# Single-query cached attention: K's loads move from SP's DMA queue to GpSimd's, one packet per DMA engine and load

## The chip, the cores and the metric

One NeuronCore of a Trainium2 chip runs the whole kernel. The metric is device time in microseconds for one execution, the lower the better. Three runs of the kernel before took 2513.58 (the median), 2513.52 and 2514.34 us. About 0.2% (5 us) is what a measurement of this kernel can tell from no change.

## The reference

One decode step: a gated mix of a cached multi-head attention (32 heads, head size 128, 65536 cached positions, one query) and a small SwiGLU block. All inputs are bfloat16.

```python
# x: [1, 1, 512]; k_cache, v_cache: [1, 32, 65536, 128]; wq: [512, 4096]; wo: [4096, 512]
q = (x @ wq) per head                                  # [1, 32, 1, 128]
p = softmax(einsum("bhqd,bhkd->bhqk", q, k_cache) * 128 ** -0.5)
a = einsum("bhqk,bhkd->bhqd", p, v_cache) as [1, 1, 4096] @ wo
b = (silu(x @ w_gate) * (x @ w_up)) @ w_down           # w_gate, w_up: [512, 1792]
g = sigmoid((x * gate_w).sum())
out = g * a + (1 - g) * b                              # [1, 1, 512]
```

Nearly all bytes are K and V: 32 heads x 2 x 16.8 MB = 1073.7 MB, of 1087.6 MB in all.

## The kernel before, in words

Each head's K and each head's V (16.8 MB) is loaded in two halves, u = 0 and u = 1 (called K_A, K_B and V_A, V_B here, with the head in brackets: K_A(r+1)). A half is 128 partitions x 64 KB = 8.39 MB, one DMA. A row is one partition's 64 KB. All four kinds lie in one buffer, `ring`, of 176 KB per partition, and overlap there: K_A is at 0 to 64 KB, K_B at 32 to 96 KB, V_A at 96 to 160 KB, V_B at 112 to 176 KB. So a half may be loaded only when enough of the half that lies across it has been used.

What each engine does for head r, in its order:

- VectorE (DVE) turns K: it waits for K_A(r), transposes it in 16 chunks into four small buffers `kt` (L314, semaphore `ktd` counts the chunks, 32 per head), then copies `psW` into `brow` (L327) and scales `psO` (L330), which ends the head before; then it waits for K_B(r), turns its 16 chunks, takes the maximum of the scores (L338) and transposes the probabilities (L340).
- TensorE (PE) makes four score matmuls per chunk (L401). After the scores of K_A(r) it works off V_B(r-1): 48 matmuls from `flow` (L417), 8 that add up `brow` (L452), 64 from `values` (L408), after which `vbd` goes up. After the scores of K_B(r) and the softmax it works off V_A(r): 48 matmuls of `flow`, after which `va1` goes up, and 16 more. PE works strictly in this order: scores of K_A(r+1) stand behind V_A(r), scores of K_B(r+1) behind V_B(r). DVE can be four chunks ahead of PE, no more.
- ScalarE (ACT) makes the exponentials, GpSimd (POOL) the two reductions over partitions per head (L216, L218), which wait for `s_mx` and `s_exp`.
- SP issues every large DMA, in one queue and in this order per head (function `head`, L167): K_A(r+1) once 8 chunks of K_B(r) are turned, V_B(r) once `va1` says that most of V_A(r) is used, K_B(r+1) once 8 chunks of K_A(r+1) are turned, V_A(r+1) once `vbd` says that V_B(r) is used. In the last such head, the two loads of `wo` stand between V_B and K_B.

The start is a special case: the query weights `wq` (4.19 MB) are issued first (L136), then head 0's K in four halves of a half. The row of x and the gate's row come through ACT's queue (L137, L232), 1 KB each. V_A(0) lies over `wq` and waits until the query is made (`s_q`). At the end, after the `wo` matmuls of heads 0 to 30 (L428, L512; semaphore `s_wod`), come the SwiGLU weights and V_B(31) in six pieces.

Of the kernel before, what the change touches and what calls it, by code (L numbers as in the profile page):

```python
# [9 lines left out]
K_A, K_B = 0, 32 * KB  # L10
# [16 lines left out]
def bass_gated_mix__mha_block_cached__swiglu_ffn__decode_kernel(  # L27
# [11 lines left out]
    out: bass.AP,  # L39
):  # L40
    _, H, S, Dh = A_k_cache.shape
    D = A_wq.shape[0]
    F = B_w_gate.shape[1]
    Dc = D // P
    FC = F // P
    ROWS = S // (2 * P)
    NCH = ROWS // CH
    SCALE = float(Dh) ** -0.5
    assert Dh == 128 and D == 512 and F % P == 0 and ROWS == 256 and H == 32
    L = H - 1  # L50
    A_ORDER = list(range(NCH // 2, NCH)) + list(range(NCH // 2))
    B_ORDER = list(range(NCH))
    PER = 2 * NCH

    with ExitStack() as ctx:
# [6 lines left out]
        def sem(name):  # L62
            return ctx.enter_context(nc.semaphore(name))
# [47 lines left out]
        sm = {n: sem(n) for n in names.split()}  # L111
# [4 lines left out]
        kv_dram = {"k": A_k_cache[0].rearrange("h (u p r) d -> h u p (r d)", u=2, p=P),  # L116
                   "v": A_v_cache[0].rearrange("h (u p r) d -> h u p (r d)", u=2, p=P)}

        def at(byte, n):
            return ring[:, byte // 2:byte // 2 + n]  # L120
# [21 lines left out]
        @block.sync  # L142
        def _(sp):
            def load(dst, src, s):
                sp.dma_start(dst, src).then_inc(sm[s], 16)  # L145

            def place(kind, h, u, s):
                byte = {"k": (K_A, K_B), "v": (V_A, V_B)}[kind][u]
                src = kv_dram[kind][:, u]
                if isinstance(h, int):  # L150
                    src = src[h]
                else:
                    src = src[bass.ds(h, 1)].rearrange("h p n -> (h p) n")
                load(at(byte, ROWS * Dh), src, s)

            k0 = kv_dram["k"][0, 0]
            k1 = kv_dram["k"][0, 1]
            half = ROWS * Dh // 2
            load(at(K_A + 2 * half, half), k0[:, half:2 * half], "s_ka")
            load(at(K_A, half), k0[:, 0:half], "s_k0a")  # L160
            load(at(K_B + 2 * half, half), k1[:, half:2 * half], "s_k0b")
            sp.wait_ge(sm["ktd"], NCH // 2)
            load(at(K_B, half), k1[:, 0:half], "s_kb")
            sp.wait_ge(sm["s_q"], 1)
            place("v", 0, 0, "s_va")

            def head(r, late):  # L167
                sp.wait_ge(sm["ktd"], r * PER + (PER - NCH // 2))
                place("k", r + 1, 0, "s_ka")
                sp.wait_ge(sm["va1"], r + 1)  # L170
                place("v", r, 1, "s_vb")
                if late:
                    wo_dram = A_wo.rearrange("(p j) n -> p (j n)", j=32)
                    for q in range(2):
                        sp.wait_ge(sm["ktd"], r * PER + (PER + 3 * NCH // 4 + q * NCH // 4))
                        load(at(WO + q * 16 * KB, 16 * D), wo_dram[:, q * 16 * D:(q + 1) * 16 * D], "s_wo")
                sp.wait_ge(sm["ktd"], r * PER + (PER + NCH // 2))
                place("k", r + 1, 1, "s_kb")
                sp.wait_ge(sm["vbd"], r + 2)
                place("v", r + 1, 0, "s_va")  # L180

            with nc.Fori(0, L - 1, engines=[ET.SP]) as i:
                head(i, False)
            head(L - 1, True)
            sp.wait_ge(sm["s_wod"], 1)
            load(at(WG, Dc * F), B_w_gate.rearrange("(p c) f -> p (c f)", c=Dc), "s_wg")
            load(at(WU, Dc * F), B_w_up.rearrange("(p c) f -> p (c f)", c=Dc), "s_wu")
            sp.wait_ge(sm["ktd"], PER * H)
            wd_dram = B_w_down.rearrange("(p c) n -> p (c n)", c=FC)
            load(at(WD, WD_CUT * D), wd_dram[:, 0:WD_CUT * D], "s_wd")  # L190
            last = kv_dram["v"][L, 1]
            for n, ((r0, r1), s) in enumerate(zip(PARTS, MARKS)):
                if n == 1:
                    sp.wait_ge(sm["va1"], H)
                load(at(V_B + r0 * 256, (r1 - r0) * Dh), last[:, r0 * Dh:r1 * Dh], s)
            for j, s in ((FC - 3, "s_wd1"), (FC - 2, "s_wd2"), (FC - 1, "s_wd3")):
                load(at(WD + 2 * j * D, D), wd_dram[:, j * D:(j + 1) * D], s)

        @block.gpsimd
        def _(pool):  # L200
            nc.gpsimd.memset(xTz[:], 0.0).then_inc(sm["s_qd"], 1)
            nc.gpsimd.memset(qd[:], 0.0).then_inc(sm["s_qd"], 1)
            for m, n in enumerate(MARKS[1:]):
                nc.gpsimd.memset(hbuf[:, m], 0.0).then_inc(sm[n], 16 * L)
            nc.gpsimd.memset(hot[:], 0.0).then_inc(sm["s_hot"], 1)
            pool.wait_ge(sm["s_id"], 1)
            pool.wait_ge(sm["s_hot"], 1)
            nc.gpsimd.tensor_copy(hot[:, 31:128:32], ident[:, P - 4:P])
            for je in range(4):
                off = 64 * (je // 2) + je % 2  # L210
                last = nc.gpsimd.tensor_copy(sel[:, je, :].rearrange("p (g d) -> p g d", g=4),
                                             ident[:, off:off + 63:2].unsqueeze(1).to_broadcast([P, 4, 32]))
            last.then_inc(sm["s_sel"], 1)
            for h in range(H):
                pool.wait_ge(sm["s_mx"], h + 1)
                nc.gpsimd.partition_all_reduce(amx, mxs, P, RMAX).then_inc(sm["s_ar"], 1)  # L216
                pool.wait_ge(sm["s_exp"], h + 2)
                nc.gpsimd.partition_all_reduce(Lt, rsum, P, RADD).then_inc(sm["s_L"], 1)  # L218

        @block.scalar  # L220
        def _(act):
# [342 lines left out]
```

## Time and profile before

| | |
|---|---|
| median of the runs | 2513.58 us (2513.52 to 2514.34) |
| the profiled execution, first to last instruction (span) | 2512.5 us |
| bytes read from HBM | 1087.64 MB, 433 GB/s over the span |
| busy share: PE, DVE, ACT, POOL | 60%, 50%, 2%, 1% |
| one head in the steady part | 77.27 us (1221.80 to 1299.07, from the issue of one K_A to that of the next) |
| granted TensorE clock, mean | 0.785 |

The page of the profile has one time for the profiled execution, its span of 2512.5 us; the 1.1 us to the median of the runs lie outside of the span. Rows of the timeline read: start, duration, engine, line, operation, output<-input, count, and in brackets how long the engine had been idle and what released it. A row SPq is a DMA issue: its duration is that of the issue, not of the transfer. In the table of stretches the columns are the stretch, its length, each engine's busy time with its count, the granted clock, the busy share of the 16 DMA engines and the rate in GB/s.

### The profile page before, as it was taken

The numbers are of one execution on the slowest core, as the hardware profiler recorded it, in microseconds if no ns is written. First come the engines' busy times: TensorE is split into PE (matmuls) and PEld (weight loads), VectorE is DVE, ScalarE is ACT, GpSimd is POOL, SyncE is SP. The second block draws the span as 40 slices with busy tenths as digits, with TensorE's granted clock in tenths as the row PEclk, the third lists the DMA queues.
The fourth block names the chain that finished last, engine by engine and source line by source line (L and its number), as shares of the span: only waits on it lengthen the run. The fifth ranks groups of instructions, "written<-read, shape, count | busy, mean of one in ns | idle before, by whom it ended". The sixth has DMA issues, their size and how long they took to land.

```text
span 2512.5 us, 25250 instructions
## 1 busy us (share of the span) xinstructions
PE 1510.1 (60%) x10158; PEld 574.4 (23%) x10158; DVE 1249.7 (50%) x1213; ACT 43.0 (2%) x142; POOL 25.9 (1%) x81
## 2 busy tenths in 40 slices
PE   5565655755656556566465565565655655656568
PEld 1222221222222222222222221222221222222222
DVE  5464553644545536446455364464553644645534
ACT  0000000000000000000000000000000000000000
POOL 0000000000000000000000000000000000000000
PEclk9877877878778777778787787777877777778779
DMA  9999999999999999999999999999999999999999
GB/s 418 434 434 434 434 434 434 434 434 434 434 434 434 434 434 434 434 434 434 434 434 434 434 434 434 436 435 435 435 435 435 434 434 435 434 436 434 434 433 395
DMA packets 20749, 1087.73 MB, mean 433 GB/s; under 512 B 2308, under 2 KB 2695, under 8 KB 2951
## 3 DMA queue, kind: packets, MB, share of 16 engines
q1 hardware_dynamic: 20736, 1087.64, 100.0%
q8 instruction: 4, 0.07, 0.0%
q14 instruction: 3, 0.02, 0.0%
q10 hardware_dynamic: 6, 0.00, 0.0%
HBM read 1087.64 MB, written 0.00 MB: 433 GB/s over the span
## 4 chain that ended last, share of the span: by engine, by line
DMA 75%; DVE 15%; issue 7%; PE 2%; DVEq 0%; SPq 0%; ACT 0%; POOL 0%
DMA ring<-in_A_k_cache_dram 74%; DVE kt L314 15%; PE psS L401 2%; DMA ring<-in_A_v_cache_dram 1%; DVEq L311 0%; SPq L145 0%; PE psW L417 0%; DVE st L325 0%; PE psY L423 0%; ACT pa L251 0%; DVE pb L340 0%; DVE st L338 0%; DVEq L324 0%; DVE fin L359 0%; SPq L136 0%
## 5 line engine op out<-in xcount | busy, mean ns | idle before, releaser
L401 PE MATMUL psS<-kt,zq 128*128 128x512 bf16 x4096 | 1132.7, 426 | 851.7 <-DVE kt L314 833.2
L314 DVE STREAM_TRANSPOSE kt<-ring 128x1024 uint32<-128x1024 uint32 x1024 | 1163.1, 1206 | 936.4 <-DMA ring<-in_A_k_cache_dram 936.4
L401 PEld LDWEIGHTS psS<-kt,zq 128*128 128x128 bf16 x4096 | 386.8, 104 | 1583.9 <-DVE kt L314 1120.7
L417 PE MATMUL psW<-ring,pb 128*4 128x512 bf16 x3584 | 253.5, 444 | 103.5 <-DVE pb L340 102.4
L417 PEld LDWEIGHTS psW<-ring,pb 128*4 128x4 bf16 x3584 | 93.9, 97 | 261.3 <-issue 184.4
L327 DVE COPY brow<-psW 128x512 f32<-128x512 f32 x32 | 22.1, 691 | 120.3 <-PE psW L417 120.3
L408 PEld LDWEIGHTS psO<-pb,ring 128*128 128x128 bf16 x2048 | 56.8, 98 | 0.6 <-DMA ring<-in_A_v_cache_dram 0.6
L408 PE MATMUL psO<-pb,ring 128*128 128x1 bf16 x2048 | 56.5, 163 | 0.4 <-DMA ring<-in_A_v_cache_dram 0.2
L330 DVE TENSOR_SCALAR lt<-psO,st,sc 128x4 f32 x32 | 9.4, 294 | 89.1 <-PE psO L408 89.1
L452 PE MATMUL psO<-id,brow 128*128 128x1 f32 x256 | 33.7, 253 | 25.6 <-DVE brow L327 24.8
L340 DVE STREAM_TRANSPOSE pb<-pa 128x512 bf16<-128x512 bf16 x32 | 22.8, 711 | 48.7 <-ACT pa L251 48.7
L249 ACT ACTIVATE st<-st 128x1 f32<-128x1 f32 x32 | 6.5, 203 | 2353.9 <-POOL st L216 2353.9
L338 DVE TENSOR_REDUCE st<-psS 128x1 f32<-128x512 f32 x32 | 22.1, 692 | 37.4 <-PE psS L401 37.4
L452 PEld LDWEIGHTS psO<-id,brow 128*128 128x128 f32 x256 | 31.0, 191 | 41.7 <-DVE brow L327 40.4
L216 POOL PARTITION_ALL_REDUCE st<-st x32 | 11.2, 351 | 2416.5 <-DVE st L338 2416.5
L251 ACT ACTIVATE pa<-psS,st 128x512 bf16<-128x512 f32 x32 | 22.0, 687 | 1.0
L428 PE MATMUL psF<-ring,om 128*1 (+1 forms) x32 | 13.1, 410 | 2.7 <-DMA ring<-in_A_wo_dram 2.7
L512 PE MATMUL psY<-ring,hot 128*128 (+1 forms) x32 | 13.6, 424 | 0.0
L218 POOL PARTITION_ALL_REDUCE st<-st x32 | 12.3, 384 | 36.4 <-ACT pa L251 36.4
L256 ACT COPY zq<-qd 128x16 bf16 x31 | 7.7, 248 | 0.0
L251 ACT ACTIVATION_READ_ACCUMULATOR pa<-psS,st 128x1 f32 x32 | 6.2, 193 | 0.0
L428 PE MATMUL psF<-ring,kt 128*1 128x512 bf16 x11 | 4.0, 542 | 2.9 <-DVE kt L353 2.9
(87 smaller groups left out, 53.2 us busy)
## 6 DMA issues: line engine op xcount, KB each, us to landing
ring<-in_A_k_cache_dram SPq DMA_DIRECT2D x4, 4096.0 KB, 27.5
ring<-in_A_v_cache_dram SPq DMA_DIRECT2D x3, 2048.0 KB, 17.3
ring<-in_A_wq_dram SPq DMA_DIRECT2D x1, 4096.0 KB, 12.3
ring<-in_A_wo_dram SPq DMA_DIRECT2D x2, 2048.0 KB, 10.5
ring<-in_B_w_gate_dram SPq DMA_DIRECT2D x1, 1792.0 KB, 20.6
ring<-in_B_w_up_dram SPq DMA_DIRECT2D x1, 1792.0 KB, 24.4
ring<-in_B_w_down_dram SPq DMA_DIRECT2D x1, 1408.0 KB, 12.8
ring<-in_A_v_cache_dram SPq DMA_DIRECT2D x1, 1280.0 KB, 20.8
```

The lines of the kernel that those rows point to most:

```text
L218: nc.gpsimd.partition_all_reduce(Lt, rsum, P, RADD).then_inc(sm["s_L"], 1)
L251: nc.scalar.activation(pa[:], psS[:], ACT.Exp, bias=nbias, scale=SCALE, accum_out=rsum).then_inc(sm["s_exp"], 1)
L314: nc.vector.transpose(o, src).then_inc(sm["ktd"], 1)
L327: nc.vector.tensor_copy(brow[:], psW[:]).then_inc(sm["s_flc"], 1)
L338: nc.vector.reduce_max(mxs, psS[:], AX_X).then_inc(sm["s_mx"], 1)
L340: nc.vector.transpose(pb[:], pa[:]).then_inc(sm["s_pb"], 1)
L401: last = nc.tensor.matmul(psS[:], zw[je][c], ktb[n % NB][:, je // 2, :, je % 2], start=first and je == 0, stop=stop and je == 3)
L408: last = nc.tensor.matmul(psO[:, 0:1], at(base + r * 256, Dh), pb[:, col:col + 1], start=first and n == 0, stop=stop and n == len(rows) - 1)
L417: last = nc.tensor.matmul(psW[g:g + 4, :], pb[:, col:col + 97:32], at(base + r * 256, 4 * Dh), start=first and n < 4, stop=stop and n >= l ...
L428: return nc.tensor.matmul(psF[0:1, :], lhs, rhs, start=first, stop=stop)
L452: nc.tensor.matmul(psO[:, 0:1], brow[:, e * Dh:(e + 1) * Dh], id4[:, e:e + 1], start=e == 0, stop=False)
L512: return nc.tensor.matmul(psY[:], hot[:, bass.ds(31 - j, P)], w, start=first, stop=stop)
```

## The change

The loads of K, but for two of the four pieces of head 0's K, are taken from SP's program and put into GpSimd's, each behind the same wait as before, and with `single_packet=True`: on each of the 16 DMA engines, one load of 8 rows (512 KB) is asked to be one packet. SP keeps `wq`, two pieces of head 0's K, all of V, and the other weights. So there are now two queues with large loads, where there was one.

```diff
@@ block.sync
-            load(at(K_A + 2 * half, half), k0[:, half:2 * half], "s_ka")
             load(at(K_A, half), k0[:, 0:half], "s_k0a")
             load(at(K_B + 2 * half, half), k1[:, half:2 * half], "s_k0b")
-            sp.wait_ge(sm["ktd"], NCH // 2)
-            load(at(K_B, half), k1[:, 0:half], "s_kb")
             sp.wait_ge(sm["s_q"], 1)
             place("v", 0, 0, "s_va")
 
             def head(r, late):
-                sp.wait_ge(sm["ktd"], r * PER + (PER - NCH // 2))
-                place("k", r + 1, 0, "s_ka")
                 sp.wait_ge(sm["va1"], r + 1)
                 place("v", r, 1, "s_vb")
...
-                sp.wait_ge(sm["ktd"], r * PER + (PER + NCH // 2))
-                place("k", r + 1, 1, "s_kb")
                 sp.wait_ge(sm["vbd"], r + 2)
                 place("v", r + 1, 0, "s_va")
@@ block.gpsimd
+            def k_load(dst, src, s):
+                nc.gpsimd.dma_start(dst, src, single_packet=True).then_inc(sm[s], 16)
+
+            half = ROWS * Dh // 2
+            k_load(at(K_A + 2 * half, half), kv_dram["k"][0, 0, :, half:2 * half], "s_ka")
             nc.gpsimd.memset(xTz[:], 0.0).then_inc(sm["s_qd"], 1)
...
+            pool.wait_ge(sm["ktd"], NCH // 2)
+            k_load(at(K_B, half), kv_dram["k"][0, 1, :, 0:half], "s_kb")
             for h in range(H):
+                if h < L:
+                    pool.wait_ge(sm["ktd"], h * PER + (PER - NCH // 2))
+                    k_load(at(K_A, ROWS * Dh), kv_dram["k"][h + 1, 0], "s_ka")
                 pool.wait_ge(sm["s_mx"], h + 1)
                 nc.gpsimd.partition_all_reduce(amx, mxs, P, RMAX).then_inc(sm["s_ar"], 1)
                 pool.wait_ge(sm["s_exp"], h + 2)
                 nc.gpsimd.partition_all_reduce(Lt, rsum, P, RADD).then_inc(sm["s_L"], 1)
+                if h < L:
+                    pool.wait_ge(sm["ktd"], h * PER + (PER + NCH // 2))
+                    k_load(at(K_B, ROWS * Dh), kv_dram["k"][h + 1, 1], "s_kb")
```

SP's queue, the loop over the heads, as it was (128x32768 is a half of K or V, 64 KB per partition):

```order
L145 ISA [waits ktd]
L145 DMA ring<-in_A_k_cache_dram 128x32768
L145 ISA [waits va1]
L145 DMA ring<-in_A_v_cache_dram 128x32768
L177 REGISTER_ALU
L145 ISA [waits ktd]
L145 DMA ring<-in_A_k_cache_dram 128x32768
L179 REGISTER_ALU
L145 DMA ring<-in_A_v_cache_dram 128x32768 [waits vbd]
```

and as it is now:

```order
L145 ISA [waits va1]
L145 DMA ring<-in_A_v_cache_dram 128x32768
L172 REGISTER_ALU
L145 ISA [waits vbd]
L145 DMA ring<-in_A_v_cache_dram 128x32768
L175 REGISTER_ALU
L175 COMPARE_AND_BRANCH
```

Both loads of K with their waits are gone from SP's loop; only V's two, with their own waits, are left.

GpSimd's program, from its last set-up copies to the end of the first head, as it was (the rows named ISA with `st` are the two reductions):

```order
L211 COPY sel<-ident 128x128 x4
L216 ISA
L216 ISA st<-st 128x1 [waits s_mx]
L218 ISA st<-st 128x1 [waits s_exp]
L216 ISA st<-st 128x1 [waits s_mx]
L218 ISA st<-st 128x1 [waits s_exp]
```

and as it is now:

```order
L209 COPY sel<-ident 128x128 x4
L195 DMA ring<-in_A_k_cache_dram 128x16384 [waits ktd]
L195 DMA ring<-in_A_k_cache_dram 128x32768 [waits ktd]
L219 ISA
L219 ISA st<-st 128x1 [waits s_mx]
L221 ISA st<-st 128x1 [waits s_exp]
L195 DMA ring<-in_A_k_cache_dram 128x32768 [waits ktd] x2
```

K_A of the next head now stands ahead of a head's two reductions, and K_B behind them; with the next head's K_A it makes the row x2.

## The prediction

> **What bounds the kernel now.** I read the page's slices and its DMA part first, then the table of stretches, then one head in the timeline. The page, and one steady head as a stretch, with the first 4 us and the last stretch:
>
> ```profile
> GB/s 418 434 434 434 434 434 434 434 434 434 434 434 434 434 434 434 434 434 434 434 434 434 434 434 434 436 435 435 435 435 435 434 434 435 434 436 434 434 433 395
> q1 hardware_dynamic: 20736, 1087.64, 100.0%
> q10 hardware_dynamic: 6, 0.00, 0.0%
> ring<-in_A_wq_dram SPq DMA_DIRECT2D x1, 4096.0 KB, 12.3
> DMA 75%; DVE 15%; issue 7%; PE 2%; DVEq 0%; SPq 0%; ACT 0%; POOL 0%
> ...
> 0.00:4.00 4.00, 0.16 (x1) 0.10 (x1) 2.22 (x13) 1.28 (x1) 1.98 (x16) 1.00 0.72 238
> 1221.80:1299.07 77.27, 44.54 (x318) 17.76 (x317) 38.73 (x38) 1.13 (x4) 0.73 (x2) 0.80 1.00 434
> 2419.60:2512.50 92.90, 77.69 (x533) 26.57 (x531) 36.26 (x38) 3.24 (x8) 0.74 (x2) 0.89 0.95 409
> ```
>
> The DMA engines are full from the first slice to the last: share 1.00 in a steady head, while PE is busy 44.54 of 77.27 us and DVE 38.73. The wait for K that leads the chain is not K being late in the queue, it is bytes. A head has four loads, so one load takes 77.27 / 4 = 19.32 us, and one of an engine's 8 rows 2.41 us. The time that is not transfer is about 5 us of the last stretch (5% of 92.9) and 1.1 us of the first four (28%).
>
> What keeps the engines full is that a load is always queued before the last one ends. One head's timeline:
>
> ```profile
> 1212.48 18.14 DVE L314 STREAM_TRANSPOSE kt<-ring 128x1024 uint32<-128x1024 uint32 x16 [12.61 <-DMA ring<-in_A_k_cache_dram]
> 1213.78 17.98 PE L401 MATMUL psS<-kt,zq 128*128 128x512 bf16 x64 [14.36 <-DVE kt L314]
> 1221.80 0.33 SPq L145 DMA_DIRECT2D ring<-in_A_k_cache_dram  x1
> 1232.58 0.35 POOL L216 PARTITION_ALL_REDUCE st<-st  x1 [75.41 <-DVE st L338]
> 1234.01 0.71 DVE L340 STREAM_TRANSPOSE pb<-pa 128x512 bf16<-128x512 bf16 x1 [1.52 <-ACT pa L251]
> 1234.07 0.38 POOL L218 PARTITION_ALL_REDUCE st<-st  x1 [1.14 <-ACT pa L251]
> 1234.95 3.63 PE L417 MATMUL psW<-ring,pb 128*4 128x512 bf16 x64 [3.19 <-DVE pb L340]
> 1237.91 0.33 SPq L145 DMA_DIRECT2D ring<-in_A_v_cache_dram  x1
> 1251.18 1.25 DVE L314 STREAM_TRANSPOSE kt<-ring 128x1024 uint32<-128x1024 uint32 x1 [16.46 <-DMA ring<-in_A_k_cache_dram]
> 1260.54 0.33 SPq L145 DMA_DIRECT2D ring<-in_A_k_cache_dram  x1
> 1270.45 2.77 PE L417 MATMUL psW<-ring,pb 128*4 128x512 bf16 x48
> 1276.70 0.33 SPq L145 DMA_DIRECT2D ring<-in_A_v_cache_dram  x1
> 1289.76 11.38 DVE L314 STREAM_TRANSPOSE kt<-ring 128x1024 uint32<-128x1024 uint32 x10 [12.65 <-DMA ring<-in_A_k_cache_dram]
> ```
>
> K_B(r) lands at 1212.4; behind it in the queue stands V_A(r), which needs 19.3 us and so lands at about 1231.7. PE wants it at 1234.95: 3 us to spare. K_A(r+1) is issued at 1221.80, 9.3 us after K_B landed, and lands at 1251.1, behind V_A. Then V_B(r) lands at about 1270.4, just when PE asks (1270.45). So V arrives in time because it stands ahead of the K issued later.
>
> **Does a second queue cut in?** The trace of before has one such place, at the start: two rows of 1 KB on ACT's queue beside `wq` on SP's.
>
> ```profile
> 0.73 0.39 SPq L136 DMA_DIRECT2D ring<-in_A_wq_dram  x1
> 1.29 0.21 ACTq L232 DMA_DIRECT2D gwrow<-in_gate_w_dram  x1
> 7.73 0.68 DVE L299 CUSTOM_DVE_ANT_0 xg<-xrow,gwrow 1x512 f32<-1x512 bf16 x1 [4.32 <-DMA gwrow<-in_gate_w_dram]
> 13.15 1.90 PE L381 MATMUL psY<-ring,xTz 128*32 128x512 bf16 x16 [4.10 <-DMA ring<-in_A_wq_dram]
> ```
>
> The gate's row is issued 0.56 us after `wq` and lands at 7.7, `wq` at 13.1. It was not held back until `wq` was through. The size fits rows taken in turn: the second queue had four packets ahead of or in this DMA (x, its semaphore, the row, its semaphore; the page counts 6 on q10 with the output's two), `wq` on SP has 8 rows per engine at 9.66 / 8 = 1.21 us (4.19 MB at 434 GB/s are 9.66 us), and the first four microseconds moved 238 x 4 = 952 KB, that is 2.2 us of work, so data begin at 1.8. 1.8 + 4 x 1.21 = 6.6, and 1.1 for the landing. I conclude that an SP load gives way to another queue at each of its rows.
>
> **The change, part by part.** *Moved issues.* 64 of the 66 issues of K go from SP to GpSimd. SP's cost 0.33 us each beside full DMA engines, so their removal is worth 0. What GpSimd needs for one is not in the trace: 0.33 us, as on SP, from below; from above I find only the 6 us from which it would decide the case (first rival), and I take the value near SP's, with 1.1 us to the first data. GpSimd is busy 0.73 us of 77.27. K_A's issue, due at 1221.80, stands ahead of the reductions at 1232.58 and 1234.07, 10 us later; K_B's, due at 1260.54, stands behind them, 26 us earlier. Neither meets them.
>
> *The order of the transfers.* This is the term. A K load that is one packet of 8 rows against V rows taken singly goes through nearly whole as soon as it is issued: K:V is 8:1. Follow one head from v, when V_A(r) has landed and PE has been waiting for it. From issue to landing on free engines a load needs its bytes and 12.3 - 9.66 = 2.64 us (the row of `wq`), 1.1 before the data and 1.5 behind (the first four microseconds).
>
> PE makes 48 matmuls, `va1` releases V_B(r). That took 1237.91 - 1234.95 = 2.96 us, but with PE warm. A PE that has waited long starts at half rate:
>
> ```profile
> 1214.19 0.15 PEld L401 LDWEIGHTS psS<-kt,zq 128*128 128x128 bf16 x1 [0.28 <-issue]
> 1214.62 0.15 PEld L401 LDWEIGHTS psS<-kt,zq 128*128 128x128 bf16 x1 [0.28 <-issue]
> 1219.31 6.64 PEld L401 LDWEIGHTS psS<-kt,zq 128*128 128x128 bf16 x30 [0.27 <-issue]
> 75.56 5.31 PE L417 MATMUL psW<-ring,pb 128*4 128x512 bf16 x64 [3.20 <-DVE pb L340]
> 76.57 0.15 PEld L417 LDWEIGHTS psW<-ring,pb 128*4 128x4 bf16 x4 [0.27 <-issue]
> 77.00 0.15 PEld L417 LDWEIGHTS psW<-ring,pb 128*4 128x4 bf16 x4 [0.27 <-issue]
> ```
>
> After 14.4 us of idleness the scores come one per 0.43 us from 1213.78 to 1219.31; the 48 then stand as 12 groups of four at 0.43, as at 76.57 and 77.00: 5.1 us with the release, against 2.96 (between them 64 took 5.31 at 75.56 and 3.63 at 1234.95). I take 5.1, since PE will have waited over 20 us. In this time no V is queued, and K_A(r+1) has long landed (below). K_B(r+1) can't be issued either: its 8 chunks need PE past V_A(r). So the engines stand idle for 2.64 + 5.1 = **7.7 us**.
>
> V_B's data begin at v + 6.2. PE is free at v + 6, DVE had four chunks ready, the eighth is turned at about v + 12, K_B(r+1) is issued, cuts in at about v + 14, and V_B, with 11.5 us left, waits 19.3: it lands at v + 6.2 + 38.6 + 1.5 = v + 46.3. PE finished the scores at v + 22 and waits. Then 1276.70 - 1270.45 = 6.25 us to `vbd`, cold 8.4 (2.1 more for the 48); K_B is in, K_A(r+2) waits for DVE, which waits for `brow` and `psO`. Idle again: 2.64 + 8.4 = **11.0 us**. V_A(r+1) starts at v + 55.8; DVE turns 8 chunks of K_B from v + 55 on, K_A is issued at v + 64.5 (9.3 later), cuts in at v + 67, is in at v + 88; V_A lands at v + 55.8 + 38.6 + 1.5 = v + 95.9. The head closes as it began, PE waiting for V, K_A in 8 us earlier. A head takes 77.27 + 7.7 + 11.0 = 96 us. Warm, the idle is 2.64 + 2.96 + 2.64 + 6.25 = 14.5 and a head 91.8.
>
> *Start and end.* PE's first V waits until `wq`, K(0), K_A(1) and V_A(0) are all in, 4.19 + 16.78 + 8.39 + 8.39 = 37.7 MB at 434 GB/s = 87 us, from 1.8, and 1.5: 90.3, where it was 75.56: +14.7. At the end:
>
> ```profile
> 2394.07 5.00 PE L417 MATMUL psW<-ring,pb 128*4 128x512 bf16 x64 [3.19 <-DVE pb L340]
> 2439.31 0.59 PE L428 MATMUL psF<-ring,om 128*1 128x512 bf16 x1 [2.65 <-DMA ring<-in_A_wo_dram]
> 2461.51 16.61 PE L401 MATMUL psS<-kt,zq 128*128 128x512 bf16 x64
> ```
>
> From V_A(30) to the end it was 2512.5 - 2394.07 = 118.4. Now V_B(30) lands at v + 46.3, `wo` follows it without a gap (4.19 MB, 9.7 us), its matmuls need 22.2 (2439.31 to 2461.51), and the rest 51.0: 129. I take +10, between 0 and 11, since V_A(31) is in early.
>
> *Sum* against the profiled execution: 2512.5 + 14.7 + 30 x 18.7 + 10 = 3098; with the 1.1 us between span and median, **3100 us**. Warm throughout it is 2512.5 + 14.7 + 30 x 14.5 + 10 + 1 = 2973; with a landing 1 us longer per V load, 60 more than the first.
>
> **The rivals.** *No cutting in, so no change (19%).* If a V load is not left before its last row, K goes behind it and the order is that of today: 2513.6. The gate's row speaks against it: it passed 8 rows of `wq`. The same comes out if GpSimd issues late. V_A's data begin 1.5 us before K_B's landing; its last row starts 7 x 2.41 = 16.9 later, 15.4 after the landing; K_A is released at 9.3. A delay of 6 us or more from release to data would do it, against 1.1 on SP. The Trainium skill, in "DMA: Bandwidth & Descriptors", section "Queues, rings and completion order", says that each engine goes round its queues by packets, of typically 9 to 17 descriptors. A V load is 8 rows and a semaphore per engine; by that it is one packet, and the time would stay at 2513.6. The gate's row disagrees, as `wq` has the same 8 rows and a semaphore.
>
> *Row for row (13%).* If the change doesn't make one packet of K, the queues share 1:1. V_A has 8 us left when K_A comes, is through 16 us later, 5 us late for PE; K_A then has 11 us left, which covers V_B's 7.7. Nothing is idle in the steady part; the start costs some of its 14.7 us, so 2514 to 2560, some 2525. The point from which it turns: K must be through before V, 19.3 us of K against 8.4 of V, so from about 2.3 rows of K for one of V on the 3100 holds.
>
> *Faster (6%).* K_B(31) no longer stands behind `wo` in SP's program, and 64 loads have fewer packet ends. All that is not transfer is about 6 us, so at best 2508, if the steady order holds as today. Against it: the engines are full in every other stretch.
>
> **How the numbers follow.** 62% for K first, which has its own range of 2960 to 3165 and is the time given. Of the 19% of no change I put 2 over +0.2%; of the 13% of sharing, 9. Within 0.2% (5 us) a measurement of this kernel can't tell a difference from none. So slower 62 + 2 + 9 = 73%, same 17 + 4 = 21%, faster 6%. The range 2511 to 3140 holds about 50 of the 62, and nearly all of the two rivals at 2513 to 2560.
>
> **What would show it.** Right: DMA share near 0.8 in a steady head of 96 us, period cut by two holes of about 8 and 11 us; PE's longest waits for V's DMA, no longer for DVE; GpSimd's K from issue to landing in about 22 us, V's in 41. Wrong: if K needs 29 us as now, it did not cut in; if both need about 30 and no hole shows, they share; a head of 77.3 us with PE never waiting for V refutes the sum.

## The result

| kernel | median | lowest to highest | profiled span | ratio to before, 95% interval |
|---|---|---|---|---|
| before | 2513.72 us | 2513.52 to 2514.34 | 2512.5 us | |
| changed | 2537.43 us | 2537.08 to 2539.49 | 2535.7 us | 1.0095 [1.0084, 1.0107] |

The changed kernel is slower by 0.95%, 23.7 us. The side was forecast rightly, the size was not: 3100 us stood for a K load that goes through nearly whole, ahead of V's rows, and no load of K does.

The first page of the changed kernel, its table of stretches for one steady head, and its DMA issues (KB of each where all are alike, and the median time from issue to landing):

```profile
GB/s 427 368 430 441 434 431 430 439 435 432 430 439 435 432 430 439 435 432 430 439 435 432 430 440 434 432 430 440 434 432 430 440 434 432 430 440 434 432 430 302
q1 hardware_dynamic: 11520, 559.16, 51.0%
q0 software_dynamic: 9216, 528.49, 48.1%
```

```profile
1312.33:1389.60 77.27, 43.60 (x314) 17.78 (x317) 38.73 (x38) 1.13 (x4) 1.83 (x4) 0.80 1.00 434
```

```profile
ring<-in_A_v_cache_dram SPq DMA_DIRECT2D x63, 29.7
ring<-in_A_k_cache_dram POOLq DMA_DIRECT2D x62, 29.0
ring<-in_A_wo_dram SPq DMA_DIRECT2D x2, 2048.0 KB, 25.0
```

K's bytes are now on GpSimd's queue q0 (528 MB) and the rest on q1. A steady head takes 77.27 us with the engines full, exactly as before. Both kinds of load need about 30 us (29.7 for V, 29.0 for K). Only two slices of the page stand out: 368 GB/s in the second and 302 in the last, where before has 434 and 395. So the 23 us are lost at the start and at the end. The list of issues points to the end too: `wo` takes 25.0 us from issue to landing (10.5 before).

**The start.** Stretches of the changed kernel (busy time of PE, PEld, DVE, ACT, POOL; then the granted clock, the DMA share and GB/s), and below them the same stretches of before:

```profile
68.00:72.00 4.00, 2.66 (x7) 1.09 (x9) 4.00 (x4) 0.00 (x0) 0.00 (x0) 0.50 0.23 98
72.00:76.00 4.00, 4.00 (x15) 1.53 (x14) 4.00 (x5) 0.00 (x0) 0.00 (x0) 0.73 0.00 0
76.00:80.00 4.00, 4.00 (x20) 1.68 (x19) 4.00 (x4) 0.00 (x0) 0.53 (x1) 1.00 0.78 262
```

```profile
68.00:72.00 4.00, 3.85 (x16) 1.14 (x16) 3.23 (x3) 0.00 (x0) 0.00 (x0) 1.00 0.91 393
72.00:76.00 4.00, 0.80 (x10) 0.21 (x12) 1.40 (x2) 1.13 (x4) 0.74 (x2) 0.98 1.13 492
76.00:80.00 4.00, 4.00 (x48) 1.54 (x44) 0.00 (x0) 0.00 (x0) 0.00 (x0) 0.60 0.85 365
```

In these 12 us the changed kernel moves (98 + 0 + 262) x 4 = 1.4 MB, before (393 + 492 + 365) x 4 = 5.0 MB: 3.6 MB less, some 8 us at 434 GB/s. The timeline of the changed kernel says why:

```profile
67.63 18.14 DVE L320 STREAM_TRANSPOSE kt<-ring 128x1024 uint32<-128x1024 uint32 x16 [22.73 <-DMA ring<-in_A_k_cache_dram]
77.06 0.53 POOL L195 DMA_DIRECT2D ring<-in_A_k_cache_dram  x1 [41.09 <-DVE kt L320]
90.11 5.32 PE L423 MATMUL psW<-ring,pb 128*4 128x512 bf16 x64 [3.20 <-DVE pb L346]
```

The lower half of K_B(0), issued at 35.43, shares the engines with V_A(0) and the upper half on SP, where one queue had given the three a fixed order. K_B(0) is in at 67.63; before it was in at 53.09:

```profile
53.09 1.25 DVE L314 STREAM_TRANSPOSE kt<-ring 128x1024 uint32<-128x1024 uint32 x1 [9.43 <-DMA ring<-in_A_k_cache_dram]
62.40 0.34 SPq L145 DMA_DIRECT2D ring<-in_A_k_cache_dram  x1
```

K_A(1) waits for eight transposed chunks of K_B(0), so its issue moves from 62.40 to 77.06. By 72 us all that was queued is through: SP has nothing that it may issue, GpSimd waits for DVE, and the engines stand idle. By the trace's DMA packets, the last row ahead of this hole begins at 69.6 and the next one at 78.3. With the bytes of these packets summed by time, the changed kernel is 8.7 us behind the kernel before from there on, by the same 8.7 (within 0.1) through 29 heads.

**The end.** In the timeline, three points from before's last 120 us, and these and three more of the changed kernel:

```profile
2410.31 1.25 DVE L314 STREAM_TRANSPOSE kt<-ring 128x1024 uint32<-128x1024 uint32 x1 [16.47 <-DMA ring<-in_A_k_cache_dram]
2424.03 4.83 SPq L145 DMA_DIRECT2D ring<-in_A_wo_dram  x2
2461.71 0.33 SPq L145 DMA_DIRECT2D ring<-in_B_w_gate_dram  x1
```

```profile
2407.26 3.63 PE L423 MATMUL psW<-ring,pb 128*4 128x512 bf16 x64 [3.24 <-DVE pb L346]
2423.40 1.25 DVE L320 STREAM_TRANSPOSE kt<-ring 128x1024 uint32<-128x1024 uint32 x1 [16.42 <-DMA ring<-in_A_k_cache_dram]
2432.89 0.57 POOL L195 DMA_DIRECT2D ring<-in_A_k_cache_dram  x1 [26.17 <-DVE kt L320]
2437.13 4.83 SPq L145 DMA_DIRECT2D ring<-in_A_wo_dram  x2
2466.95 0.58 PE L434 MATMUL psF<-ring,om 128*1 128x512 bf16 x1 [17.29 <-DMA ring<-in_A_wo_dram]
2488.56 0.33 SPq L145 DMA_DIRECT2D ring<-in_B_w_gate_dram  x1
```

The first matmul with V_A(30) comes at 2407.26, 13.2 us later than the 2394.07 of before: 8.7 us from the start, and some 4.5 because K lands about two rows later than its place in the bytes would have it. (K_A(31): 2423.40 against 2410.31 is the same 13.1.) The trace's packets show these two rows in a steady head: on three of the engines one row of V runs from 1217.7 to 1220.1, ahead of K_B's last row, and a second from 1222.6 to 1225.0, ahead of the packet that raises K_B's semaphore, and DVE starts at 1225.62. From V_A(30) to the end it is then 2535.7 - 2407.26 = 128.4 us, against 118.4. Here `wo` shares with K_B(31), issued 4 us ahead of it and no longer behind it. PE waits 17.3 us for `wo`, the gate's weights wait for PE's work with `wo` and are issued at 2488.56 instead of 2461.71, and the engines run dry twice:

```profile
2482.00:2490.00 8.00, 7.93 (x28) 2.50 (x29) 0.53 (x1) 0.59 (x1) 0.00 (x0) 1.00 0.39 155
2496.00:2504.00 8.00, 7.69 (x30) 2.32 (x29) 7.11 (x7) 0.00 (x0) 0.00 (x0) 1.00 0.35 151
```

That closes the account: 13.2 + 10.0 = 23.2 us of span. By bytes, the lag of 8.7 us grows over these two holes to 19.7 at the end of the last transfer (2529.8 against 2510.0), and the other 3.5 are work of PE behind it.

**How the two queues share.** The DMA queues of two stretches of the changed kernel (packets, MB, share of 16 engines); first 6 to 18 us, where K and `wq` both have rows of 32 KB, then 2440 to 2458, where K's rows are 64 KB and `wo`'s 16 KB:

```profile
q1 hardware_dynamic: 80, 2.62, 50.5%
q0 software_dynamic: 79, 2.59, 49.9%
```

```profile
q0 software_dynamic: 96, 6.29, 80.6%
q1 hardware_dynamic: 96, 1.57, 20.4%
```

80 to 79, and 96 to 96: one row of one queue for one of the other, whatever their sizes. No K load goes through whole. This is the row-for-row rival of the prediction. In a steady head the two queues hardly meet: from 1239.5 to 1254 us GpSimd's queue moves 96 rows of K, and SP's only 8 packets of V's semaphores. Rows of both stand side by side only for a row or two, where one load ends and the next begins.

### The profile page after: what moved, and what is told of

Its sections match the earlier page's. It is cut to its first block, busy times and chain, and to the rows that moved or that the text cites. A ratio compares the mean times of both kernels' runs of the same rounds, so it can differ in the third digit from the quotient of the medians.

```text
span 2535.7 us, 25001 instructions
## 1 busy us (share of the span) xinstructions
PE 1482.2 (58%) x10029; PEld 576.5 (23%) x10158; DVE 1250.1 (49%) x1213; ACT 43.1 (2%) x142; POOL 61.3 (2%) x145
## 4 chain that ended last, share of the span: by engine, by line
DMA 73%; DVE 15%; issue 8%; PE 4%; DVEq 0%; ACT 0%; POOL 0%; POOLq 0%
DMA ring<-in_A_k_cache_dram 72%; DVE kt L320 15%; PE psS L407 2%; DMA ring<-in_A_wo_dram 1%; PE psF L434 1%; DVEq L317 0%; PE psY L518 0%; PE psW L423 0%; DVE st L331 0%; PE psY L494 0%; DVE kt L354 0%; PE psO L414 0%; PE psY L429 0%; PE psO L458 0%; ACT pa L257 0%
## 5 line engine op out<-in xcount | busy, mean ns | idle before, releaser
L407 PE MATMUL psS<-kt,zq 128*128 128x512 bf16 x3968 | 1101.9, 423 | 870.5 <-DVE kt L320 848.1
L423 PE MATMUL psW<-ring,pb 128*4 128x512 bf16 x3584 | 258.9, 452 | 114.1 <-DVE pb L346 102.5
L195 POOL DMA_DIRECT2D ring<-in_A_k_cache_dram x64 | 35.4, 553 | 2022.7 <-DVE kt L320 2021.9
L434 PE MATMUL psF<-ring,om 128*1 (+1 forms) x32 | 12.8, 399 | 17.8 <-DMA ring<-in_A_wo_dram 17.3
```

Source lines behind the costliest of these rows:

```text
L195: nc.gpsimd.dma_start(dst, src, single_packet=True).then_inc(sm[s], 16)
L407: last = nc.tensor.matmul(psS[:], zw[je][c], ktb[n % NB][:, je // 2, :, je % 2], start=first and je == 0, stop=stop and je == 3)
L423: last = nc.tensor.matmul(psW[g:g + 4, :], pb[:, col:col + 97:32], at(base + r * 256, 4 * Dh), start=first and n < 4, stop=stop and n >= l ...
L434: return nc.tensor.matmul(psF[0:1, :], lhs, rhs, start=first, stop=stop)
```

## The experiments

Ratios are to the kernel before, run beside each on the same chip (2513.68, 2514.04 and 2513.71 us).

**Without the flag.** The changed kernel with the option on K's loads left out.

```diff
-                nc.gpsimd.dma_start(dst, src, single_packet=True).then_inc(sm[s], 16)
+                nc.gpsimd.dma_start(dst, src).then_inc(sm[s], 16)
```

> The changed kernel without single_packet=True, all else the same. Theory A (the two queues take turns row by row, and the flag makes no packet of K's 8 rows): nothing changes, 2537 us +- 3, and at the start K's and the other queue's 32 KB rows are moved in equal numbers, as with the flag. Theory B (the flag does make one packet per engine, but K comes too late in the steady part to cut in): without it K's rows are moved otherwise wherever the queues overlap, at the start and beside wo at the end, and the time moves by more than 5 us.

Measured: 2538.27 us (2535.75 to 2540.23), 1.0100 [1.0083, 1.0117]. In the stretch from 6 to 18 us its queues show

```profile
q0 software_dynamic: 80, 2.62, 50.5%
q1 hardware_dynamic: 80, 2.62, 50.5%
```

The same time and the same turns: the flag has no effect here that the time or the order shows. What the change does to the time it does by the second queue.

**The first head back on SP.** Head 0's K goes out on SP in the old order, all but the last 256 bytes per partition of two pieces, which GpSimd still issues.

```diff
             load(at(K_B + 2 * half, half), k1[:, half:2 * half], "s_k0b")
+            load(at(K_A + 2 * half, half - Dh), k0[:, half:2 * half - Dh], "s_k0c")
...
+            sp.wait_ge(sm["ktd"], NCH // 2)
+            load(at(K_B, half - Dh), k1[:, 0:half - Dh], "s_k0d")
...
-            k_load(at(K_B, half), kv_dram["k"][0, 1, :, 0:half], "s_kb")
+            k_load(at(K_B + 2 * half - 2 * Dh, Dh), kv_dram["k"][0, 1, :, half - Dh:half], "s_kb")
...
```

> Head 0's K goes back to SP in the order of the kernel before, but for 256 bytes per partition of each of the two pieces, which GpSimd still loads; K of heads 1 to 31 stays on GpSimd. Theory A (the loss is a hole of some 9 us at the start, where all loads in flight were through and K_A(1) was not yet issued, and two holes of 11 us in all at the end, with 3 us of PE work behind): the hole at the start goes, 2537.4 - 8.7 = 2529 us, and K_A(1) is issued near 62 us instead of 77. Theory C (the steady part loses by the second queue, and the start only shows it first): no more than 3 us are won, 2534 or more, and a head takes over 77.4 us.

Measured: 2530.53 us (2529.02 to 2532.06), 1.0065 [1.0048, 1.0081]; span 2530.6. Two rows of its timeline, and a stretch at the place of the first hole:

```profile
62.62 0.54 POOL L198 DMA_DIRECT2D ring<-in_A_k_cache_dram  x1 [28.11 <-DVE kt L323]
2415.21 1.25 DVE L323 STREAM_TRANSPOSE kt<-ring 128x1024 uint32<-128x1024 uint32 x1 [16.37 <-DMA ring<-in_A_k_cache_dram]
```

```profile
70.00:78.00 8.00, 2.38 (x9) 0.62 (x8) 2.75 (x4) 1.13 (x4) 0.74 (x2) 0.87 1.15 500
```

K_A(1) is issued at 62.62 again (62.40 before) and the hole is gone: the bytes are 0.0 to 0.7 us behind the kernel before through all steady heads. 6.9 us came back in the medians, where the hole had cost 8.7: in the profiled run the two holes at the end are larger, some 14 us in all by the bytes, where the changed kernel has some 12. The second row separates the two parts of the delay at the end: K_A(31) still lands 4.9 us after the 2410.31 of before though the bytes are on time. That is two rows of 2.41 us, the two of V described above.

**`wo` ahead of K_B(31) on one queue.** The changed kernel with `wo`'s two loads moved from SP to GpSimd, under the same waits, before the issue of K_B(31): the order of before for these three loads.

```diff
...
+                if h == L - 1:
+                    wo_dram = A_wo.rearrange("(p j) n -> p (j n)", j=32)
+                    for q in range(2):
+                        pool.wait_ge(sm["ktd"], h * PER + (PER + 3 * NCH // 4 + q * NCH // 4))
+                        k_load(at(WO + q * 16 * KB, 16 * D), wo_dram[:, q * 16 * D:(q + 1) * 16 * D], "s_wo")
                 if h < L:
                     pool.wait_ge(sm["ktd"], h * PER + (PER + NCH // 2))
                     k_load(at(K_B, ROWS * Dh), kv_dram["k"][h + 1, 1], "s_kb")
```

> The two loads of wo go to GpSimd's queue too, behind the waits that they have, ahead of K_B(31), so that the three stand in one queue in the order of the kernel before. Theory A (wo's 16 KB rows take turns with K_B(31)'s 64 KB rows, so wo's matmuls, the release of the SwiGLU weights and the end come later): wo's first matmul comes about 14 us earlier against V_A(30), and the time is 2537.4 - 11.3 - 3.2 = 2523 us. Theory D (wo's matmuls are not on the path that sets the end): 2535 to 2539.

Measured: 2543.12 us (2542.4 to 2544.1), 1.0118 [1.0101, 1.0135]. It was to win and it lost 5.7 us on the changed kernel. Its timeline:

```profile
2450.55 0.59 PE L434 MATMUL psF<-ring,om 128*1 128x512 bf16 x1 [0.60 <-DMA ring<-in_A_wo_dram]
2488.22 18.14 DVE L320 STREAM_TRANSPOSE kt<-ring 128x1024 uint32<-128x1024 uint32 x16 [38.61 <-DMA ring<-in_A_k_cache_dram]
```

The first half of the reasoning held: PE has `wo` at 2450.55 instead of 2466.95. But K_B(31), now behind `wo`, takes turns with V_A(31) on SP and lands at 2488.2, where the changed kernel has it at 2461.4. The hole moved behind it. In both orders one load is late, the one into which the other queue puts its rows.

**Both of these.** The edits of the last two together.

> Both of the edits before: head 0's K back on SP but for 256 bytes per partition of two pieces, and wo on GpSimd ahead of K_B(31). K and V of heads 1 to 31 are in two queues as in the change. Theory A (the two queues cost and bring nothing in the steady part): 2514 us, within 0.2% of the kernel before. Theory C (the second queue itself costs): 2520 or more. A gain of the second queue, by fewer packet ends or an earlier K, would show as 2511 or less.

Measured: 2533.59 us (2532.2 to 2536.15), 1.0079 [1.0062, 1.0096], not the 2514 that I expected. Against the run with `wo` moved alone it is 9.5 us less: the start again, where the hole had cost 8.7. What is left has the same reason as there, K_B(31) behind `wo`:

```profile
2480.69 18.14 DVE L323 STREAM_TRANSPOSE kt<-ring 128x1024 uint32<-128x1024 uint32 x16 [39.79 <-DMA ring<-in_A_k_cache_dram]
```

**Both ends on SP.** The first head as in the second experiment, and K_B(31) on SP behind `wo`, as before, all but its last 256 bytes per partition. Only the 30 steady heads are left to two queues.

```diff
...
                         load(at(WO + q * 16 * KB, 16 * D), wo_dram[:, q * 16 * D:(q + 1) * 16 * D], "s_wo")
+                    sp.wait_ge(sm["ktd"], r * PER + (PER + NCH // 2))
+                    load(at(K_B, (ROWS - 1) * Dh), kv_dram["k"][r + 1, 1, :, 0:(ROWS - 1) * Dh], "s_k31")
...
-                    k_load(at(K_B, ROWS * Dh), kv_dram["k"][h + 1, 1], "s_kb")
+                    lo = (ROWS - 1) * Dh if h == L - 1 else 0
+                    k_load(at(K_B + 2 * lo, ROWS * Dh - lo), kv_dram["k"][h + 1, 1, :, lo:ROWS * Dh], "s_kb")
...
```

> Start and end as in the kernel before: head 0's K, and K_B(31) behind wo, come from SP in the old order, but for one row of 256 bytes per partition of three of these pieces, which GpSimd loads. K of heads 1 to 30 and K_A(31) stay on GpSimd. Theory A (the steady part neither loses nor wins by two queues that take turns row by row): 2514 us, within 0.2% of the kernel before, a head of 77.3 us. Theory C (the second queue costs in itself): 2520 or more. A gain would show as 2508 or less.

Measured: 2516.62 us (2514.32 to 2517.97), 1.0010 [1.0001, 1.0019]. One head of it, and its two rows near the end:

```profile
1312.33:1389.60 77.27, 48.75 (x314) 18.20 (x312) 38.72 (x38) 1.13 (x4) 1.83 (x4) 0.76 1.00 434
```

```profile
2414.92 1.25 DVE L326 STREAM_TRANSPOSE kt<-ring 128x1024 uint32<-128x1024 uint32 x1 [16.31 <-DMA ring<-in_A_k_cache_dram]
2428.65 4.83 SPq L145 DMA_DIRECT2D ring<-in_A_wo_dram  x2
```

20.8 of the 23.7 us are back with 30 heads still on two queues: the steady part costs nothing, the ends cost nearly all. Most of the 2.9 left is at one place: K_A(31) lands the two rows late (2414.92 against 2410.31), so `wo` goes out at 2428.65 instead of 2424.03, and the engines run partly dry from 2428 to 2430. By bytes the run is 0.3 us behind the kernel before up to 2426 and 2.5 behind it from 2434 on.

**V in rows of 8 KB.** The changed kernel with V's loads (all but the six pieces at the end) cut into descriptors of 8 KB, K's still 64 KB. A descriptor is one piece of the load, in the trace one packet; so far each was a whole row. If the queues alternate by descriptors, K now really goes 8:1 in bytes, the condition of the forecast.

```diff
-            def load(dst, src, s):
-                sp.dma_start(dst, src).then_inc(sm[s], 16)
+            def load(dst, src, s, cut=None):
+                sp.dma_start(dst, src, max_dma_last_dim=cut).then_inc(sm[s], 16)
...
-                load(at(byte, ROWS * Dh), src, s)
+                load(at(byte, ROWS * Dh), src, s, 8 * KB if kind == "v" else None)
```

> The changed kernel with V's loads (all but the six pieces at the end) cut into descriptors of 8 KB, so that a row of V is 8 of them, while a row of K stays one of 64 KB. Theory A (turns are taken descriptor by descriptor, whatever their size): K now gets 8 bytes for one of V as soon as it comes, so the prediction's case of K going first holds here: holes behind V's loads, PE waiting for V, a head of 90 to 96 us and 2920 to 3100 us. Theory E (turns are shared by bytes or time): 2537 +- 10, a head of 77.3. Theory F (K comes too late to overlap V at all): also 2537 +- 10, but no descriptor of V between K's.

Measured: 3118.39 us, 1.2404 [1.2368, 1.2440]. The queues from 1268 to 1280 us; the head; its two holes; and who waits:

```profile
q0 software_dynamic: 72, 4.72, 90.7%
q1 hardware_dynamic: 71, 0.58, 11.4%
```

```profile
1202.20:1298.55 96.35, 45.62 (x309) 17.47 (x314) 38.81 (x37) 1.13 (x4) 1.84 (x4) 0.71 0.82 348
1202.20:1212.20 10.00, 7.09 (x121) 4.14 (x123) 2.67 (x4) 0.00 (x0) 0.00 (x0) 0.67 0.10 20
1251.70:1257.70 6.00, 5.96 (x64) 1.92 (x64) 0.00 (x0) 0.00 (x0) 0.00 (x0) 0.59 0.00 0
```

```profile
PE psW L423 <- DMA ring<-in_A_v_cache_dram: 1449.3, 62, 25.2
```

72 rows of 64 KB go against 71 of 8 KB. The head is 96.35 us, with two holes of some 10 us (behind V_B) and 7 us (behind V_A; the stretch of 6 us is its empty middle), and PE waits for V twice in each head. That is the head of 96 us that I had worked out for the changed kernel.

**V in rows of 8 KB on one queue.** The same cut in the kernel before, for the price of the descriptors themselves.

> The kernel before (one queue) with the same 8 KB descriptors for V, as the price of the descriptors alone. All theories: 8 times as many descriptors for half of the bytes, 7 x 8 x 2 per engine and head at 5 ns or less each, so a head of 77.3 to 77.9 us and 2514 to 2532 us. Over 2600 would mean that e5 says nothing on turns.

Measured: 2530.2 us, 1.0064 [1.0041, 1.0087]. Its one queue:

```profile
q1 hardware_dynamic: 77184, 1087.64, 100.4%
```

56448 more packets than the 20736 of before, 3528 per engine, cost 16.2 us: 4.6 ns each. So of the 604 us of the last experiment only some 16 are the descriptors themselves; the rest is the order.

**V in rows of 32 KB.** K:V is 2:1; the prediction put the turn at "about 2.3 rows of K for one of V".

```diff
...
-                load(at(byte, ROWS * Dh), src, s)
+                load(at(byte, ROWS * Dh), src, s, 32 * KB if kind == "v" else None)
```

> The changed kernel with V's loads cut into descriptors of 32 KB, K's rows of 64 KB: K gets two bytes for one of V's while both are there. Theory A with the prediction's limit (K must get more than about 2.3 to 1 to be through before V and leave holes): no holes in the steady part, a head of 77.3 to 79 us, 2530 to 2600. Theory H (any lead of K over V is enough): a head over 85 us, 2800 or more.

Measured: 3018.48 us, 1.2008 [1.1986, 1.2030]. One head; the queues from 1307.4 to 1336.4 us, where a load of K and one of V are both under way; and two rows of the timeline, the first matmul with V_A and the first transpose of the K_A behind it:

```profile
1243.81:1338.23 94.42, 47.63 (x312) 18.00 (x312) 38.80 (x37) 1.13 (x4) 1.83 (x4) 0.72 0.83 355
```

```profile
q0 software_dynamic: 128, 8.39, 66.7%
q1 hardware_dynamic: 128, 4.19, 33.5%
```

```profile
1291.42 6.35 PE L423 MATMUL psW<-ring,pb 128*4 128x512 bf16 x64 [19.20 <-DMA ring<-in_A_v_cache_dram]
1293.92 1.25 DVE L320 STREAM_TRANSPOSE kt<-ring 128x1024 uint32<-128x1024 uint32 x1 [18.73 <-DMA ring<-in_A_k_cache_dram]
```

128 to 128 in rows, 2:1 in bytes, and that is enough. The limit of 2.3 asked that K be through before V_A. Here V_A lands 2.5 us before K_A, and the head has its holes all the same: it is enough that K ends soon after V, before PE has worked V off and the next V is issued. Between 1:1 and 2:1 the limit was not sought.

**K in rows of 16 KB, with and without the flag.** The other way round, K:V 1:4, and with 32 descriptors per engine and load for the flag to join.

```diff
-                nc.gpsimd.dma_start(dst, src, single_packet=True).then_inc(sm[s], 16)
+                nc.gpsimd.dma_start(dst, src, single_packet=True, max_dma_last_dim=16 * KB).then_inc(sm[s], 16)
```

> The changed kernel with K's loads cut into descriptors of 16 KB, 32 per engine and load, with single_packet=True. Theory A (the flag makes no packet): as the next run, within 3 us, K's descriptors of 16 KB taking turns with V's of 64 KB, so that K gets one byte for four of V while both are there. Theory B (the flag makes one packet): a K load that meets V goes through without a row of V between, and the two runs differ by over 5 us.

> The same without single_packet=True. Theory A: the same time as the run with the flag, within 3 us, and K landing later than in the change wherever V is in flight, a head of 77.3 to 80 us and 2530 to 2620 us. Theory B: differs from the run with the flag by over 5 us.

Measured: 2883.33 us (2880.84 to 2885.82) with the flag, 1.1469 [1.1436, 1.1503]; 2887.39 (2873.62 to 2901.16) without, 1.1485 [1.1356, 1.1615]. The waits, with the flag:

```profile
DVE kt L320 <- DMA ring<-in_A_k_cache_dram: 1296.1, 64, 38.3
```

No difference by the flag. The size was far off what I expected: now K is the one that gives way, DVE waits for it 1296 us in all (917 in the changed kernel), and the loss is 370 us. The price of the smaller descriptors themselves was not measured for K; at the 4.6 ns of the one queue it would be some 7 us, by my estimate (24 more descriptors per engine in each of 64 loads). In both directions an uneven share is dear.

**K in two loads of 64 partitions, with and without the flag.** Four descriptors per engine and load, in case eight are more than one packet may hold.

```diff
-                nc.gpsimd.dma_start(dst, src, single_packet=True).then_inc(sm[s], 16)
+                for e in range(2):
+                    nc.gpsimd.dma_start(dst[e:P:2], src[e:P:2], single_packet=True).then_inc(sm[s], 16)
...
-                dve.wait_ge(sm["s_ka"], i * 16 + 16)
+                dve.wait_ge(sm["s_ka"], i * 32 + 32)
...
```

> The changed kernel with each of GpSimd's K loads split into two DMAs, one for the even and one for the odd partitions, of 64 descriptors each (4 per engine), with single_packet=True. Theory G (the flag works where the whole DMA has no more than 64 descriptors): K's rows go in fours, K gets 4:1 against V, and by the prediction's sum, which needs K to be more than 2.3 to 1, the time is 2920 to 3130 us. Theory A (the flag makes no packet here either): 2535 to 2560, as the next run.

> The same two DMAs per K load without single_packet=True. All theories: K's and V's rows take turns one by one, 2535 to 2560 us.

Measured: 2543.42 us (2542.75 to 2544.09) with the flag, 1.0118 [1.0099, 1.0136]; 2542.27 (2541.8 to 2542.74) without, 1.0113 [1.0095, 1.0132]. From 6 to 18 us both show

```profile
q0 software_dynamic: 96, 2.62, 50.6%
q1 hardware_dynamic: 80, 2.62, 50.5%
```

that is, equal bytes (the 16 more on q0 are the packets of the first half's semaphore). So it is not that eight rows are too many for a packet. Why two loads cost 5 us more than one was not followed.

## Why the prediction was wrong

**The step that failed** is "A K load that is one packet of 8 rows against V rows taken singly goes through nearly whole as soon as it is issued: K:V is 8:1." K does not go through whole: its rows and SP's go 80 to 79, and with the flag and without it the kernel takes 2537.4 and 2538.3 us. The step put 18.7 us of idleness into each of 30 heads; the steady head measured 77.27 us, which is none. K needs 29.0 us and V 29.7, the prediction's own signs of sharing. Nor does the flag change anything at 4 descriptors per engine (2543.4 and 2542.3) or at 32 (2883 and 2887). I had read the packet from the change's words and never asked for a row that bears it out; the 62% rested on that. Why the flag does nothing is open: whether no packet is made, or one is made and the engines take turns inside it, no run here shows.

**The sum behind it was right**, under its own condition. Where K:V was made 8:1 by the size of V's descriptors, a head took 96.35 us (96), its holes some 7 and 10 us (7.7 and 11.0), V needed 41.4 us from issue to landing (41) and the kernel 3118 (3100). K needed 26.9 us, where I had 22.

**That an SP load gives way at every row**, read from the gate's row, was right: 80 rows to 79. The count behind it was not, so that its 7.7 us came out is luck. By the packets of the trace of before, x's row and its semaphore are through by 1.7 us, ahead of `wq`'s first row; the gate's row moves at 6.1 and its semaphore at 7.4, with one row of `wq` (6.16 to 7.37) between them. Why the gate's row waited until 6.1 is open. On this the Trainium skill, "DMA: Bandwidth & Descriptors", section "Queues, rings and completion order", says that an engine drains a packet of typically 9 to 17 descriptors before it goes to the next queue; by that the time would have stayed at 2513.6. The traces differ: descriptors of 8, 16, 32 and 64 KB each were a turn of their own (72 to 71, 96 to 96, 80 to 79), and the time is 2537.4.

**The start term**, +14.7, came near only by luck. V's first matmul came at 90.11, where I had 90.3; but it waits for the softmax behind K_B(0), which shared with V_A(0), and not for a K_A(1) that went ahead. And as a term of the whole time it was too large: the start costs the 8.7 us of the hole. **The end term**, +10, measured 128.4 - 118.4 = 10.0, by luck as well: `wo` is late because K_B(31) is queued beside it, not because V_B(30) lands late.

**The row-for-row rival** had the mechanism, with "Nothing is idle in the steady part", and "2514 to 2560, some 2525". In the steady part V was not even the 5 us late that the prediction gave it. Its first row slips in before the last of the K that is under way, and it has only a row or so left when the next K comes; it needs 29.7 us from issue to landing, against 32.2 before, and PE's V matmul still waits for DVE and not for a DMA:

```profile
1248.15 5.32 PE L423 MATMUL psW<-ring,pb 128*4 128x512 bf16 x64 [3.24 <-DVE pb L346]
```

Its 2525 holds some 11 us, all for the start, and nothing for the end; the hole's 8.7, K's two rows (4.5) and the end's 10.0 make the 23.2 that were measured. The account of a rival deserves the same care as that of the forecast: each place where two loads now meet, the last loads too.

**No cutting in** (2513.6) fell as the gate's row said: rows of both queues take turns. Nor does GpSimd issue late. Its issue takes some 0.55 us, not 0.33, and lies beside full engines; K_A(1), issued at 77.06 on idle engines, shows its first data at 78.3, 1.2 us after the issue, where I took 1.1. **Faster** had at best 2508; the fewest microseconds of any order tried here were the 2513.7 of one queue.

**The point from which it turns** was too high: 2.3 by the prediction, 2 or less by the run with 32 KB. Its condition, K through before V, was too strict: there V_A landed before K_A, and the holes came.

## What to carry to other kernels

Where the DMA engines are full, as here, a second queue brought no bandwidth (434 GB/s in a steady head either way) and changed only which load lands first. One queue in the order of need lands the first needed load first; in two queues that take turns, that load lands late by the other's rows. Look then at the places where the chain has no spare load queued, here the first loads and the last ones, and find the holes in a table of stretches. And where two queues do meet, compare the sizes of their descriptors before anything else: the queue whose rows are twice as large got twice the bytes (8.39 to 4.19 MB).

## What the hardware showed that I had not expected

GpSimd's queue and SP's take turns by single descriptors, so the size of a descriptor is a priority. At equal sizes, with loads that hardly meet, the second queue cost nothing in a steady head (77.27 us); 8:1 for K cost the kernel 24%, 2:1 for K still 20%, 1:4 against K 15%. On one queue the same cut into 8 KB costs 0.6%, 4.6 ns for each descriptor more.

A load's semaphore takes a turn of its own as well: K_B's packet of 4 bytes waits at 1222.6 for a whole row of V and goes at 1225.0.

The option that is to make one packet of a GpSimd load had no effect on order or time at 4, 8 or 32 descriptors per engine. What it does change, no run here shows.
